# Four transformer-like layers on one core: loads, layer normalisation and some matmuls put in another order

## The chip, the cores and the metric

The kernel runs on one core of a Trainium2 chip. The metric is the time of one execution on the device, in microseconds (us), taken as the median of several executions. One execution of each kernel was also recorded by the hardware profiler; all readings of "the trace" and "the profile" below are from such single executions.

The engines are called as the profile calls them: PE is TensorE, DVE is VectorE, ACT is ScalarE, POOL is GpSimd, SP is the engine that issues the loads and stores (DMA). "L260" is a line of the kernel in question; the numbers differ from kernel to kernel.

## The reference

```python
S, D, F = 2048, 576, 4608            # bf16 inputs, 32 heads of 18

def A(x, wqkv, wo):                   # linear attention
    q, k, v = split(x @ wqkv)
    phi = lambda t: where(t > 0, t + 1, exp(t)) + 1e-6
    pq, pk = phi(q), phi(k)
    kv, z = einsum(pk, v), sum(pk)    # summed over all 2048 tokens
    return merge_heads(pq @ kv / (pq @ z + 1e-6)) @ wo

def B(x, w1, b1, w2, b2):             # MLP; it normalises its input once more
    return gelu(layernorm(x) @ w1 + b1) @ w2 + b2

x = x + A(layernorm(x), wqkv, wo)
x = x + B(layernorm(x), w1, b1, w2, b2)
x = x + A(layernorm(x), wqkv, wo)     # the same weights again
x = x + B(layernorm(x), w1, b1, w2, b2)
```

An attention layer has two passes, because `kv` needs all tokens before the first output can be made: a key/value pass (16 tiles of 128 tokens: normalise, transpose, project to k and v, accumulate), then a second pass (queries, output, projection with `wo`).

## The kernel before

All loads go through one queue, in the order of their issue by SP. Weights for later layers ("late pieces") are issued two per tile in the first key/value pass.

```python
load_x0(0); load_x0(1)
load_kd(wqkv_sb, A_wqkv, nc.sync)          # all three parts: q, k, v
load_x0(2); load_x0(3)
for i in range(NWARM):                     # 10 matmuls that only warm the clock
    nc.tensor.matmul(warm_ps[:], lhsT=ident[:], rhs=x0_tiles[0][:, 0:512], start=True, stop=True)
# ...
late_pieces = [piece_wo] + [w1 in 9 pieces] + [w2 in 6 pieces] + [piece_bias]   # abridged
#   piece_bias: load b1, cast it on DVE to b1T; load b2, cast it on DVE to b2_bc

def ln_part1(key, xt, kind, norm_eng):     # one tile's normalisation, all at once
    nc.vector.bn_stats(...); nc.vector.bn_stats(...); nc.vector.bn_aggr(...)    # ln_st, ln_mv
    nc.vector.tensor_scalar(...)                                                # ln_u = var + eps
    nc.gpsimd.tensor_tensor(out=rstd[:], in0=u[:], in1=neg_half[:], op=ALU.pow) # ln_rstd
    nc.vector.tensor_scalar(out=nmr[:], ...)                                    # ln_nmr = -mean * rstd
    # y_ring[...] = x * rstd + nmr on ACT (tiles 0 to 3) or POOL (the others)

def ln_part2(key, t, evac_eng):            # transpose, then copy out of PSUM
    # five PE transposes into tp (a single buffer), then
    # yT[..., t] = tp on DVE (first layer)

# key/value pass, first layer, before tile t:
#   load x of tile t+4, ln_part1 of tile t+4, ln_part2 of tile t+2, two late pieces
# kv_proj(t): PE k_ps -> ACT exp and identity -> DVE pk; PE v_ps -> ACT and DVE v_ring
# residual: two DVE additions of 288 columns each
```

v_ps is a single PSUM buffer. PE can write it for the next tile only after ACT and DVE have copied the last tile's value into v_ring.

## Time and profile before

| | before |
|---|---|
| median | 835.68 us (4 executions, 833.95 to 836.19) |
| profiled execution | 833.95 us, span 832.2 us, mean granted clock 0.995 |
| PE busy | 98% |

The first two parts of the page of the kernel before; the second line is the granted TensorE clock in tenths, in 40 slices of the span.

```profile
PE 813.1 (98%) x7154; PEld 672.7 (81%) x7154; DVE 297.1 (36%) x1034; ACT 410.1 (49%) x864; POOL 100.7 (12%) x148
...
PEclk8999999999999999999999999999999999999999
```

PE is the limit, and nearly all of its time is needed. So the question is where the other 2% lie, plus the time at a slow clock, which counts as busy. The view by windows of the kernel before, cut at the first key matmul (15.00 us), the start of the second pass (75.14), the first MLP's first output matmul (122.53) and the second attention layer's start (427.87):

```profile
core 0: us, PE busy (x) PEld busy (x) DVE busy (x) ACT busy (x) POOL busy (x), PEclk, DMA share, GB/s
0.00:15.00 15.00, 5.47 (x20) 2.55 (x21) 5.07 (x21) 3.23 (x4) 11.72 (x44) 0.90 0.90 280
15.00:75.14 60.14, 57.88 (x508) 45.21 (x506) 44.27 (x177) 37.90 (x94) 17.68 (x24) 0.97 0.74 204
75.14:122.53 47.39, 45.85 (x416) 34.36 (x416) 44.25 (x180) 31.79 (x56) 5.50 (x5) 1.00 0.43 139
122.53:427.87 305.34, 304.99 (x2716) 259.56 (x2714) 84.43 (x231) 134.83 (x283) 33.19 (x41) 1.00 0.14 45
```

Each row begins with its limits, then its length, then busy time by engine. The MLP row has 0.35 us to give; the first 75 us have the most.

The waits of PE in the first 128 us of the kernel before (who waited, for whom, sum, times, longest):

```profile
PE tp L186 <- DVE yT L190: 6.4, 1, 6.4
...
PE tp L186 <- POOL y_ring L178: 2.2, 3, 0.9
PE tp L186 <- ACT y_ring L174: 1.1, 2, 0.7
```

The large one is at the start. DVE's timeline of the kernel before shows why (start, length, what; the bracket is the idle time ahead of it and its end):

```profile
12.02 0.46 DVE L156 BATCH_NORM_STATS2 ln_st<-xbf 128x6 f32<-128x288 bf16 x1 [5.94 <-DMA xbf<-in_A_x_dram]
...
13.98 0.48 DVE L190 COPY yT<-tp 128x640 bf16<-128x640 bf16 x1
```

DVE stands 5.94 us in front of the third tile's statistics, because that tile's load is queued behind `wqkv`. The copy of the first transposed tile stands behind those statistics in DVE's order, and the second transpose, which needs the same PSUM buffer, waits for the copy. The Trainium skill says so in general ("TensorE: Matmul & The Clock Gate", Part 1, on engine queues): VectorE and ScalarE take their instructions strictly first in, first out. This trace agrees: the copy's input was ready at about 8 us (the first transposes start at 7.33) and it ran at 13.98 us.

### The profile page before, as it was taken

How to read it: one execution, taken by the hardware profiler on the slowest of the kernel's cores; microseconds unless marked ns; L12 is line 12 of the kernel's file. 1: busy time of each engine (PE TensorE's matmuls, PEld its weight loads, DVE VectorE, ACT ScalarE, POOL GpSimd, SP SyncE). 2: the span in 40 equal slices, each digit the busy share in tenths (PEclk: the TensorE clock that was granted, in tenths of full speed). 3: DMA queues.
4: the chain of work that ended last, by engine and by line, in shares of the span. 5: the costliest groups of instructions: out<-in, count | busy, mean ns of one | idle time of the engine just before them, and what ended most of it. 6: DMA issues, size and time to landing. Idle time of an engine off the chain costs nothing.

```text
span 832.2 us, 17608 instructions
## 1 busy us (share of the span) xinstructions
PE 813.1 (98%) x7154; PEld 672.7 (81%) x7154; DVE 297.1 (36%) x1034; ACT 410.1 (49%) x864; POOL 100.7 (12%) x148
## 2 busy tenths in 40 slices
PE   5989999999999999999999999999999999999998
PEld 3767688888888888888877867888888888888886
DVE  4777982324150505132134589551303010000000
ACT  3667653444444444444457776344444444444443
POOL 6330200112020202020000000211011010101000
PEclk8999999999999999999999999999999999999999
DMA  9970541202020202021010026721112010101010
GB/s 291 327 166 8 171 159 59 85 2 86 2 86 1 87 1 87 18 69 56 3 58 1 2 70 208 237 72 44 36 38 72 15 44 1 45 1 44 1 30 15
DMA packets 41009, 58.21 MB, mean 70 GB/s; under 512 B 7840, under 2 KB 24480, under 8 KB 40928
## 3 DMA queue, kind: packets, MB, share of 16 engines
q1 hardware_dynamic: 40928, 57.09, 22.2%
q8 instruction: 56, 0.92, 0.5%
q14 instruction: 25, 0.20, 0.1%
HBM read 40.56 MB, written 16.52 MB: 69 GB/s over the span
## 4 chain that ended last, share of the span: by engine, by line
PE 82%; issue 4%; DVE 4%; DMA 1%; POOL 1%; POOLq 0%; ACT 0%; DVEq 0%; SPq 0%
PE h_ps L421 34%; PE m_ps L406 30%; PE wo_ps L374 4%; PE q_ps L278 4%; PE k_ps L246 3%; PE tp L186 2%; PE v_ps L257 2%; PE v_ps L254 1%; PE to_ps L364 1%; PE nd_ps L329 1%; POOL ln_rstd L167 1%; PE kvacc L270 1%; DMA xo<-x_d 1%; DVE xn L227 1%; DVE y_ring L178 1%
## 5 line engine op out<-in xcount | busy, mean ns | idle before, releaser
L424 ACT ACTIVATE hT<-h_ps,b1T 128x256 bf16<-128x256 f32 x576 | 273.2, 474 | 340.2 <-PE h_ps L421 333.2
L421 PE MATMUL h_ps<-yT,w_sb 128*128 128x256 bf16 x2880 | 407.5, 273 | 0.0
L406 PE MATMUL m_ps<-w_sb,hT 128*128 128x288 bf16 x2304 | 370.4, 286 | 0.0
L421 PEld LDWEIGHTS <-w_sb 128*128 128x128 bf16 x2880 | 279.5, 98 | 44.6
L406 PEld LDWEIGHTS <-hT 128*128 128x128 bf16 x2304 | 225.4, 98 | 42.6
L190 DVE COPY yT<-tp 128x640 bf16<-128x640 bf16 x60 | 29.1, 486 | 273.5 <-PE tp L186 273.4
L167 POOL TENSOR_TENSOR ln_rstd<-ln_u,neg_half 128x1 f32<-128x1 f32 x64 | 36.2, 566 | 504.0 <-DVE ln_u L162 273.7
L216 POOL TENSOR_TENSOR xo<-xo,b_bc 128x576 f32<-128x576 f32 x32 | 44.7, 1403 | 185.4 <-DMA xo<-x_d 185.4
L278 PE MATMUL q_ps<-yT,wqkv_sb 128*126 128x512 bf16 (+1 forms) x200 | 53.8, 381 | 0.0
L374 PE MATMUL wo_ps<-wo_sb,oT 128*128 128x288 bf16 x320 | 46.4, 286 | 0.1
L246 PE MATMUL k_ps<-wqkv_sb,yT 128*128 128x288 bf16 x320 | 46.3, 291 | 0.0
L227 DVE TENSOR_TENSOR xn<-m_ps,xo 128x288 f32<-128x288 f32 x32 | 13.3, 437 | 76.5 <-PE m_ps L406 76.5
L186 PE MATMUL tp<-ident,y_ring 128*128 128x128 bf16 x320 | 29.3, 224 | 11.4 <-DVE yT L190 6.7
L374 PEld LDWEIGHTS <-oT 128*128 128x128 bf16 x320 | 30.8, 98 | 9.9 <-ACT oT L366 1.0
L186 PEld LDWEIGHTS <-y_ring 128*128 128x128 bf16 x320 | 22.9, 100 | 19.4 <-issue 7.9
L227 DVE TENSOR_TENSOR xbf<-m_ps,xo 128x288 bf16<-128x288 f32 x32 | 12.4, 450 | 68.9 <-issue 35.7
L246 PEld LDWEIGHTS <-yT 128*128 128x128 bf16 x320 | 30.3, 99 | 7.7
L178 DVE TENSOR_SCALAR y_ring<-xn,ln_rstd,ln_nmr 128x576 bf16<-128x576 f32 x44 | 35.1, 798 | 0.6
L199 ACT ACTIVATE phi_e<-q_ps 126x512 bf16<-126x512 f32 (+1 forms) x40 | 23.9, 596 | 22.3 <-PE q_ps L278 19.8
L199 ACT ACTIVATE phi_e<-k_ps 128x288 bf16<-128x288 f32 x64 | 26.6, 416 | 11.2 <-PE k_ps L246 7.4
L202 DVE TENSOR_SCALAR phi_e<-phi_e 128x288 bf16<-128x288 bf16 (+2 forms) x104 | 27.7, 268 | 11.3 <-ACT phi_e L199 11.3
L278 PEld LDWEIGHTS <-wqkv_sb 128*126 128x126 bf16 (+1 forms) x200 | 23.8, 131 | 8.2
(70 smaller groups left out, 530.9 us busy)
## 6 DMA issues: line engine op xcount, KB each, us to landing
x_d<-xn SPq DMA_DIRECT2D x48, 288.0 KB, 2.2
xo<-x_d SPq DMA_DIRECT2D x48, 288.0 KB, 3.0
xn<-x_d SPq DMA_DIRECT2D x28, 288.0 KB, 3.3
w_sb<-in_B_w_dram SPq DMA_DIRECT2D x6, 864.0 KB, 9.3
xbf<-in_A_x_dram SPq DMA_DIRECT2D x32, 144.0 KB, 2.8
w_sb<-in_B_w_dram SPq DMA_DIRECT2D x9, 512.0 KB, 6.8
out_dram<-xbf SPq DMA_DIRECT2D x16, 144.0 KB, 1.8
wqkv_sb<-in_A_wqkv_dram SPq DMA_DIRECT2D x1, 1728.0 KB, 9.0
```

The source lines that it names most:

```text
L167: nc.gpsimd.tensor_tensor(out=rstd[:], in0=u[:], in1=neg_half[:], op=ALU.pow)
L178: eng.tensor_scalar(out=y[:, 0:D], in0=xt[:, 0:D], scalar1=rstd[:, 0:1], scalar2=nmr[:, 0:1], op0=ALU.mult, op1=ALU.add)
L186: nc.tensor.transpose(out=tp[:, k, :], in_=y[:, k * P:(k + 1) * P], identity=ident[:])
L199: nc.scalar.activation(out=e[0:rows, 0:n], in_=ps_ap, func=ACT.Exp)
L216: nc.gpsimd.tensor_tensor(out=xo[:], in0=xo[:], in1=b2_bc[:], op=ALU.add)
L227: nc.vector.tensor_tensor(out=xn[:, half * HALF:(half + 1) * HALF], in0=halves[half], in1=xo[:, half * HALF:(half + 1) * HALF], op=ALU.add)
L246: nc.tensor.matmul(kp[:, 0:HALF], lhsT=yT[:, k, tok], rhs=wqkv_sb[:, k, D + half * HALF: D + (half + 1) * HALF], start=(k == 0), stop=(k = ...
L278: nc.tensor.matmul(qp[0:GR[g], :], lhsT=wqkv_sb[:, k, GO[g]:GO[g] + GR[g]], rhs=yT[:, k, c * CA:(c + 1) * CA], start=(k == 0), stop=(k == ...
L374: nc.tensor.matmul(wp[:, half, 0:HALF], lhsT=oT[:, k, :], rhs=wo_sb[:, k, half * HALF:(half + 1) * HALF], start=(k == 0), stop=(k == KD - 1))
L406: nc.tensor.matmul(accs[j][:, half, 0:HALF], lhsT=hT[:, j * P:(j + 1) * P], rhs=w2_sb[:, f, half * HALF:(half + 1) * HALF], start=(f == 0) ...
L421: nc.tensor.matmul(hp[:, 0:CB], lhsT=w1_sb[:, k, f * P:(f + 1) * P], rhs=yT[:, k, ctok], start=(k == 0), stop=(k == KD - 1))
L424: nc.scalar.activation(out=hT[:], in_=hp[:, 0:CB], func=ACT.Gelu_apprx_tanh, bias=b1T[:, f:f + 1], scale=1.0)
```

## The change

The change intends to let matmuls start earlier and to keep DVE and POOL from making PE wait in the first attention layer. Its core, with cuts:

```diff
-NWARM = 10
+NWARM = 14
+# every start-up load is chained to the one before it, so that the scheduler keeps the order
-        load_x0(0)
-        load_x0(1)
-        load_kd(wqkv_sb, A_wqkv, nc.sync)
-        load_x0(2)
-        load_x0(3)
+        for t in range(6):
+            load_x0(t)                                  # six x buffers instead of four
+        chained(nc.sync.dma_start(out=wqkv_sb[:, 0:4, D:3 * D], ...))   # k and v columns only
+        chained(nc.sync.dma_start(out=wqkv_sb[0:64, 4, D:3 * D], ...))
-            nc.tensor.matmul(warm_ps[:], lhsT=ident[:], rhs=x0_tiles[0][:, 0:512], ...)
+            nc.tensor.matmul(warm_ps[:], lhsT=ident[:], rhs=y_ring[NY - 1][:, 0:512], ...)
-        late_pieces = [piece_wo] + [w1 ...] + [w2 ...] + [piece_bias]          # two per tile
+        late_pieces = [piece_q, piece_wo] + [w1 ...] + [w2 ...] + [piece_b1_dma]  # one per tile
+        # b2 is loaded four tiles before the end of the pass; both casts at the last tile:
+        def bias_casts():
+            nc.vector.tensor_copy(out=b1T[:], in_=bias_stage.pop("b1")[:])
+            nc.vector.tensor_copy(out=b2_bc[:], in_=bias_stage.pop("b2")[:])
-        def ln_part1(...) / def ln_part2(...)
+        class LNPipe:          # one stage of each tile per tick:
+            # 0 statistics, 1 ln_rstd, 2 ln_nmr, 3 y_ring, 4 transpose and copy
+            # stage 0 of later tiles: bn_stats ordered after the last value copy (state['vcopy'])
-            ln_part2 of the first layer: copy on DVE, two tiles ahead
+            feed(x0_tiles.pop(k), k, "A", l0_norm_eng(k), "act")   # copy on ACT, fed five tiles ahead
-            for half in range(2): nc.vector.tensor_tensor(... 288 columns ...)
+            nc.vector.tensor_tensor(... 576 columns in one ...)
             while q0:
                 q_proj(*q0.pop(0))
+            q_proj(0, 1)       # two query projections moved ahead of the second pass
+            q_proj(1, 1)
+        # up to eight of the MLP's first products (h_ps) are issued in the attention's last four tiles
```

The diff shows the order of the program. When the kernel is built, a scheduler orders each engine's instructions once more, and the traces show where it differs.

## The prediction

> **What bounds the kernel now.** TensorE. The page shows PE busy 813.1 of 832.2 us (98%). In the timeline, matmuls follow each other at 109 ns (256 columns) and 122 ns (288 columns) through both MLP layers. Summing that steady spacing over all matmuls after the warm-up gives about 801 us (estimate from the trace). So only some 30 us of the span can move at all:
> - Start-up: the first key projection (k_ps) starts at 15.00 us, and the window view grants only half the clock from about 13 to 19.8 us (k_ps spaced 240 ns). About 2 us of the work after 15 us is lost to that.
> - First attention layer, key/value pass: 2.9 us of PE gaps, 2.6 of them before transposes (tp) at 49, 55 and 58 us, waiting for POOL's y_ring.
> - Its second pass: about 2.8 us. Second attention layer: about 2.1 + 1.6 us. MLP layers: about 1 us.
> - Tail: 4.3 us after the last matmul starts.
>
> **What the change does.** It reorders. Matmul work is the same but for 4 more warm-up matmuls. It
> 1. loads six x tiles and only the K and V columns of wqkv first,
> 2. moves layer 0's yT evacuations from VectorE (486 ns) to ScalarE (693 ns),
> 3. cuts LayerNorm into stages spread over ticks,
> 4. emits two q projections early and up to 8 MLP products ahead,
> 5. merges the two residual adds (437 ns each) into one (estimate 0.75 us).
>
> **Start-up, costed.** Before, VectorE sits 5.94 us in front of tile 2's statistics, because that tile's load queued behind wqkv (landed after 9.0 us); the evacuation of tile 0 stands behind them, so tp waits 6.4 us for it. That wait goes. But the instruction order of the new kernel puts all six tiles' statistics ahead of the first ln_nmr. At about 0.91 us a tile from 3.02 us, ln_nmr of tile 0 comes near 8.6 us (5.35 before). ScalarE then does four normalisations (0.81 us apart) before the first evacuation, near 12.1 us; the second transpose waits for it, and k_ps starts near 13.2 us. So the start gains about 1.8 us, not the 5 us that the DMA order (K,V landed near 9.3 us, estimate) would allow. PE is idle from about 9 to 12.8 us except for one transpose group, so the clock may drop again. The Trainium skill ("TensorE: Matmul & The Clock Gate", Part 1) says that the clock is halved until a busy window of about 3.4 us; the trace agrees (warm-up matmuls 427 ns apart[...]). I count 1.2 us of the 2.
>
> **The sum.** Start -1.8, clock -1.2, y_ring gaps -2.2 (x tiles come six ahead, VectorE loses an evacuation per tile), second pass -1.4, MLP -0.5, second attention layer -1.3, tail -0.1: about -8.5 us. ScalarE gains 16 x 0.69 us off the critical path (66% busy at 20 to 40 us).
>
> **Predicted: 827 us, 80% range 821 to 832.** Faster by over 2%: 0.03; within 2%: 0.955; slower by over 2%: 0.015.
>
> **What would show it.** Timeline: first k_ps at 12.5 to 14 us; first ln_nmr near 8.6 us; the four normalisations ahead of the first yT copy. Waits: no tp waiting over 0.5 us for y_ring at 49 to 60 us. MLP stages within 0.5 us of before. PE busy again at 98% or more.
>
> **What would make it wrong.** If k_ps starts near 10 us with a full clock, the time falls to about 822 us. If ScalarE, now holding the evacuations behind its exponentials, makes PE wait for the single tp buffer, the key/value pass loses what it gained. If the x loads, now chained behind weight pieces, hold VectorE at statistics, the first attention layer gets longer.

## The result

| | before | after |
|---|---|---|
| median | 835.57 us (16 executions, 833.24 to 839.05) | 830.82 us (11 executions, 829.78 to 832.51) |
| profiled execution | 833.95 us, span 832.2 | 829.44 us, span 827.7 |

The ratio of after to before is 0.994, with a 95% interval of 0.9927 to 0.9953. A ratio here is the mean time of one kernel's runs over that of the other's of the same rounds, so it is not quite the ratio of the medians quoted. The chip was not the same in all batches (the kernel before had medians of 834.9, 836.64 and 835.98 us in the three batches of experiments), so experiments are best compared by their ratios to before.

The view by windows of the changed kernel, cut at the same events:

```profile
0.00:12.67 12.67, 6.18 (x25) 2.66 (x25) 6.82 (x32) 5.00 (x6) 10.10 (x37) 0.92 0.72 220
12.67:72.62 59.95, 58.60 (x508) 45.79 (x507) 39.38 (x152) 45.28 (x108) 20.23 (x25) 0.96 0.85 233
72.62:122.10 49.48, 48.91 (x440) 36.73 (x440) 44.08 (x166) 33.91 (x59) 5.62 (x5) 1.00 0.40 133
122.10:423.68 301.58, 301.58 (x2690) 257.02 (x2688) 79.08 (x213) 133.00 (x280) 35.76 (x41) 1.00 0.14 44
```

The start is 2.33 us shorter, the key/value pass only 0.19 us. The other rows can't be compared by length, as the change moved matmuls from the MLP (2716 to 2690) to the second pass (416 to 440). For that I sum, over the matmuls of a stage, the distance to the next matmul less N/2.4 + 2.5 ns for N columns. That is the full-rate spacing which the Trainium skill gives ("TensorE: Matmul & The Clock Gate", Part 1); the traces agree (109 ns at 256 columns, 122 ns at 288). What is left is pauses and slow clock. It goes from 5.40 to 5.00 us in the first key/value pass, from 2.68 to 2.01 in its second pass, from 1.02 to 0.22 in the first MLP, from 2.17 to 1.93 and from 1.41 to 1.30 in the second attention layer, and from 0.06 to 0.22 in the last MLP.

The waits of PE in the first 128 us of the changed kernel:

```profile
PE tp L240 <- ACT yT L242: 2.4, 1, 2.4
PE v_ps L311 <- DVE v_ring L318: 1.3, 2, 1.0
PE tp L240 <- ACT y_ring L228: 1.0, 1, 1.0
PE to_ps L425 <- DVE o_ring L404: 0.5, 1, 0.5
```

The waits for POOL's y_ring are gone. The start went as the prediction had it: ACT's timeline of the changed kernel has four normalisations ahead of the first copy,

```profile
8.42 3.14 ACT L228 ACTIVATE y_ring<-xbf,ln_nmr,ln_rstd 128x576 bf16<-128x576 bf16 x4 [4.04 <-DVE ln_nmr L220]
11.46 0.67 ACT L242 COPY yT<-tp 128x640 bf16<-128x640 bf16 x1
```

and PE's timeline of the changed kernel has the second group of transposes, released by that copy, and the first key matmul:

```profile
12.18 0.69 PE L240 MATMUL tp<-ident,y_ring 128*128 128x128 bf16 x5 [2.39 <-ACT yT L242]
12.67 1.65 PE L303 MATMUL k_ps<-wqkv_sb,yT 128*128 128x288 bf16 x6
```

But there is a new wait of v_ps for v_ring, and DVE's timeline of the changed kernel shows a stop that the kernel before does not have:

```profile
56.54 0.31 DVE L262 TENSOR_TENSOR pk<-phi_a,phi_e 128x288 bf16<-128x288 bf16 x1
58.51 0.18 DVE L171 CAST b1T<-b_raw 128x36 f32<-128x36 bf16 x1 [1.66 <-DMA b_raw<-in_B_b_dram]
58.61 0.23 DVE L260 TENSOR_SCALAR phi_e<-phi_e 128x288 bf16<-128x288 bf16 x1
```

The same place in DVE's timeline of the kernel before, where the cast follows without a stop:

```profile
53.50 0.44 DVE L157 BATCH_NORM_STATS2 ln_st<-xbf 128x6 f32<-128x288 bf16 x1
53.98 0.18 DVE L143 CAST b1T<-b_raw 128x36 f32<-128x36 bf16 x1
```

The load of b1 is 9 KB, but it is the last in a queue of weights, and it goes as 4608 packets of 2 bytes. It landed at 53.96 us before and at 58.49 us after: 4.5 us later, while the computation runs 2.3 us earlier. By the packets' times, the changed kernel's load was issued at 45.46 us, its first packet started at 52.49 us, its last ended at 56.04 us, and 2.4 us later it had landed. The view by windows of the changed kernel shows the queue ahead of these packets and while they run (the last number is GB/s):

```profile
44.40:52.40 8.00, 7.50 (x68) 5.72 (x67) 5.97 (x22) 7.17 (x18) 3.43 (x4) 1.00 1.09 356
52.40:56.10 3.70, 3.15 (x30) 2.53 (x30) 2.75 (x11) 2.33 (x6) 1.50 (x2) 1.00 1.17 69
```

Before, it was issued 2.0 us earlier and waited 4.0 us for its first packet, not 7.0. The traces show one reason for the delay: in the changed kernel the load of the seventh x tile is not issued before 9.31 us, since its buffer is free only when tile 0 is normalised, and all later loads are chained behind it. From 8 to 12 us the queue moved 197 GB/s, before the change 319. No run isolates this, and none loads b1 earlier or in larger packets.

In this execution the stop at 58.5 us itself costs PE little: the pauses of v_ps are at 51.6 us (1.17 us) and 55.8 us (0.45 us), ahead of it. They stand with the other thing that makes DVE stop, ln_nmr waiting up to 0.67 us a tile for POOL's ln_rstd. This stop is not new. DVE's waits from 15 to 72 us, in the kernel before and then in the changed kernel:

```profile
DVE ln_nmr L169 <- POOL ln_rstd L167: 5.8, 12, 0.7
DVE ln_nmr L220 <- POOL ln_rstd L216: 6.0, 10, 0.7
```

What is new is that PE waits for v_ps behind it. But this profiled execution is the fastest of the twelve of the changed kernel, and it ran 4.83 us after its first key matmul at half clock, so it came late to the b1 load. Would an execution that comes earlier wait longer? The times fit that: the three executions at the lowest mean clock (0.995) took 829.44, 829.78 and 830.13 us, the four at the highest (0.998) 829.96 to 831.76 us, so a fuller clock brought no time.

### The profile page after: what moved, and what is told of

It is laid out like the page before. It is cut to its first block, busy times and chain, and to the rows that moved or that the text cites. A ratio compares the mean times of both kernels' runs of the same rounds, so it can differ in the third digit from the quotient of the medians.

```text
span 827.7 us, 17553 instructions
## 1 busy us (share of the span) xinstructions
PE 814.5 (98%) x7158; PEld 673.4 (81%) x7158; DVE 286.4 (35%) x955; ACT 420.1 (51%) x880; POOL 104.5 (13%) x141
## 4 chain that ended last, share of the span: by engine, by line
PE 87%; issue 4%; DVE 1%; DMA 0%; ACT 0%; POOLq 0%; DVEq 0%; POOL 0%; SPq 0%
PE h_ps L469 36%; PE m_ps L486 32%; PE wo_ps L435 5%; PE q_ps L335 4%; PE k_ps L303 3%; PE tp L240 2%; PE v_ps L314 2%; PE v_ps L311 1%; PE to_ps L425 1%; PE nd_ps L390 1%; PE kvacc L327 1%; DMA xo<-x_d 0%; POOLq L626 0%; DVE xn L284 0%; DVE xbf L284 0%
## 5 line engine op out<-in xcount | busy, mean ns | idle before, releaser
L469 PE MATMUL h_ps<-yT,w_sb 128*128 128x256 bf16 x2880 | 403.0, 273 | 0.0
L244 DVE COPY yT<-tp 128x640 bf16<-128x640 bf16 x44 | 21.6, 490 | 241.5 <-PE tp L240 241.5
L435 PE MATMUL wo_ps<-wo_sb,oT 128*128 128x288 bf16 x320 | 52.3, 286 | 0.0
L335 PE MATMUL q_ps<-yT,wqkv_sb 128*126 128x512 bf16 (+1 forms) x200 | 51.5, 381 | 0.0
L284 DVE TENSOR_TENSOR xn<-m_ps,xo 128x576 f32<-128x576 f32 x16 | 11.4, 753 | 92.9 <-PE m_ps L486 92.9
L284 DVE TENSOR_TENSOR xbf<-m_ps,xo 128x576 bf16<-128x576 f32 x16 | 11.4, 752 | 87.8 <-PE m_ps L486 51.9
L427 ACT COPY oT<-to_ps 128x640 bf16<-128x640 bf16 x32 | 22.1, 691 | 19.3 <-PE to_ps L425 19.0
L232 DVE TENSOR_SCALAR y_ring<-xn,ln_rstd,ln_nmr 128x576 bf16<-128x576 f32 x44 | 31.2, 709 | 0.6
```

The costliest lines, as they stand in the source:

```text
L232: eng.tensor_scalar(out=y[:, 0:D], in0=xt[:, 0:D], scalar1=it["rstd"][:, 0:1], scalar2=it["nmr"][:, 0:1], op0=ALU.mult, op1=ALU.add)
L335: nc.tensor.matmul(qp[0:GR[g], :], lhsT=wqkv_sb[:, k, GO[g]:GO[g] + GR[g]], rhs=yT[:, k, c * CA:(c + 1) * CA], start=(k == 0), stop=(k == ...
L435: nc.tensor.matmul(wp[:, half, 0:HALF], lhsT=oT[:, k, :], rhs=wo_sb[:, k, half * HALF:(half + 1) * HALF], start=(k == 0), stop=(k == KD - 1))
L469: nc.tensor.matmul(hp[:, 0:CB], lhsT=w1_sb[:, k, f * P:(f + 1) * P], rhs=yT[:, k, ctok], start=(k == 0), stop=(k == KD - 1))
```

## The experiments

The theories were these. (1) What the change gains at the start it partly gives back, since DVE, which works in order, stops in the key/value pass for the bias load and for POOL. (2) Rivals: the start is limited by ACT's new copies or by the clock, and removing those limits gives the whole gain; or the moves in the second pass don't give what I had counted.

Twelve kernels ran, in three batches; all gave correct results. Each is an edit of the changed kernel. In the first batch (3 rounds) the kernel before had a median of 834.9 us.

### evac_dve: the first layer's copies back on DVE

```diff
-            lnp.feed(x0_tiles.pop(t), t, "A", l0_norm_eng(t), "act")
+            lnp.feed(x0_tiles.pop(t), t, "A", l0_norm_eng(t), "dve")
```
(the same for the tiles fed in the pass)

> The changed kernel, with layer 0's yT evacuations back on VectorE. Theory (the order of VectorE's queue decides the start): the first evacuation now stands behind the statistics of tile 6, whose load lands at about 12.4 us, so the first k_ps moves from 12.67 to about 13.9 us, and the key/value pass of layer 0 gets no shorter: about 1 to 3 us slower than the changed kernel (831.8 to 834), ratio to the kernel before 0.996 to 0.998. Rival (ScalarE's four normalisations alone hold the start): k_ps at about 11.5 us and 1 us or more faster than the changed kernel.

Measured: 831.93 us (830.1 to 832.45, 4 executions), ratio 0.9955 (0.9928 to 0.9982). The first key matmul starts at 13.87 us, 1.2 us later than in the changed kernel: the second transposes wait 3.6 us for DVE's copy. The v_ps matmuls then pause 2.65 us at 57.4 us, where DVE stands 4.2 us for b1, which lands at 59.53 us. So ACT's copies are worth about a microsecond at the start. The two pauses of v_ps at 51.6 and 55.8 us, which the changed kernel has, are absent here. The time itself differs from the changed kernel's by less than the intervals allow to tell.

### warm26: 26 warm-up matmuls instead of 14, from a buffer of their own

```diff
-NWARM = 14
+NWARM = 26
-        nc.vector.memset(y_ring[NY - 1][:], 0.0)
+        warm_src = const.tile([P, 512], BF16, name="warm_src")
+        nc.vector.memset(warm_src[:], 0.0)
+        nc.vector.memset(y_ring[NY - 1][:, D:DPAD], 0.0)
-            ... rhs=y_ring[NY - 1][:, 0:512] ...
+            ... rhs=warm_src[:] ...
```

> The changed kernel with 26 warm-up matmuls on a tile of their own instead of 14 on y_ring 3. They fill TensorE to about 10.8 us and need nothing that the start-up chain needs. Theory (the dip of the clock is a cost of its own): k_ps still starts at 12.5 to 12.9 us, no half clock after about 7.3 us, k_ps spaced 122 ns from the first one; 1.9 to 2.6 us faster than the changed kernel, ratio to before 0.991. Rival (with a full clock PE only waits for VectorE and ScalarE in those first tiles): clock full but under 1 us gained.

Measured: 836.73 us (834.71 to 837.5, 4 executions), ratio 1.0013 (0.9985 to 1.0041): as slow as the kernel before, though it did what it was to do. Its first key matmul starts at 12.68 us, as in the changed kernel, and at the full clock. The key/value pass then took 66.6 us instead of 59.95. DVE's timeline of warm26:

```profile
55.80 0.31 DVE L264 TENSOR_TENSOR pk<-phi_a,phi_e 128x288 bf16<-128x288 bf16 x1
59.92 0.18 DVE L173 CAST b1T<-b_raw 128x36 f32<-128x36 bf16 x1 [3.81 <-DMA b_raw<-in_B_b_dram]
60.01 0.23 DVE L320 CAST v_ring<-v_ps 128x72 bf16<-128x72 f32 x1
```

PE's timeline of warm26, at the same place:

```profile
60.29 1.21 PE L313 MATMUL v_ps<-wqkv_sb,yT 128*128 128x252 bf16 x5 [4.27 <-DVE v_ring L320]
```

Here the copy that frees v_ps stands behind the cast. And the stop is paid twice: the view by windows of warm26 grants half the clock in the two stretches after it (the column after POOL).

```profile
55.91:59.32 3.41, 0.11 (x1) 0.00 (x0) 0.20 (x1) 0.86 (x3) 0.00 (x0) 1.00 0.60 121
59.32:62.73 3.41, 2.44 (x11) 1.63 (x11) 1.22 (x6) 0.00 (x0) 0.00 (x0) 0.50 0.46 139
62.73:66.14 3.41, 3.41 (x22) 2.48 (x21) 0.72 (x3) 1.98 (x4) 0.00 (x0) 0.50 0.00 0
```

There was another stop of v_ps, 2.08 us at 46.5 us, where DVE waited 2.5 us for the b2 load. An earlier, faster computation meets loads that are no earlier.

### front2: the first two tiles served first

The first two tiles go through all stages before the statistics of tiles 2 to 5 (both halves) and before their normalisations; POOL's clearing of padding comes after its first ln_rstd.

```diff
-        for t in range(LEAD):
-            ...
+        for t in range(2):
+            lnp.feed(x0_tiles.pop(t), t, "A", l0_norm_eng(t), "act")
+        lnp.drain()
+        for t in range(2, LEAD):
             lnp.feed(x0_tiles.pop(t), t, "A", l0_norm_eng(t), "act")
+            lnp.items[-1]['after'] = state['nmr1']        # statistics after tile 1's ln_nmr
+            lnp.items[-1]['norm_after'] = state['evac1']  # normalisation after tile 1's copy
             lnp.tick()
+        ...                                           # two more ticks
```

> The changed kernel with tiles 0 and 1 put first on VectorE and ScalarE: their ln_nmr before the statistics of tiles 2 to 5, their evacuations before normalisations 2 and 3. Loads as in the changed kernel. Theory (queue order first, then the landing of the K and V columns): ln_nmr of tile 0 near 5.4 us, both evacuations done by about 10.2 us, k_ps then waits for the weights that landed at 11.5 and 12.2 us in the changed kernel: k_ps at 11.5 to 12.2 us, 0.5 to 1.2 us gained, clock as before or better. Rival (queue order is all): k_ps near 10 us, 2.5 us or more gained.

Measured: 829.6 us (828.95 to 831.92, 4 executions), ratio 0.9936 (0.9908 to 0.9965), the same as the changed kernel. The first key matmul came at 11.88 us, now held by the k and v weights (landed at 11.84 us), and the clock stayed full to the end of the work. Yet the pass ended at 72.72 us, in the changed kernel at 72.62. PE's waits from 10 to 75 us in front2:

```profile
PE v_ps L317 <- DVE v_ring L324: 3.9, 2, 3.0
PE k_ps L309 <- DMA wqkv_sb<-in_A_wqkv_dram: 2.4, 1, 2.4
```

All that was saved at the start was lost at 56 us, where DVE stood 4.7 us for b1.

### front2_x4: front2 with the k and v weights ahead of x tiles 4 and 5

```diff
-        for t in range(6):
+        for t in range(4):
             load_x0(t)
         ... k and v columns of wqkv ...
+        for t in range(4, 6):
+            load_x0(t)
```
(and the statistics of tiles 4 and 5 come after tile 3's ln_nmr)

> As front2, and the loads of tiles 4 and 5 behind the K and V columns. Theory (both limits lifted): weights land about 1 us sooner than in front2 (10.3 to 11.2 us), k_ps follows at 10.3 to 11.3 us, TensorE's gap before it is under 1.5 us, so the clock stays full in most runs: 3 to 5 us faster than the changed kernel, ratio to before 0.988 to 0.991. Rival (the weights' last packets land near 11.5 us whatever stands before them): k_ps at 11.5 us and over, clock dips, 1 us or less.

Measured: 831.6 us (831.27 to 834.88, 4 executions), ratio 0.9968 (0.9932 to 1.0004). The first key matmul starts at 10.30 us, the earliest of all runs, and the pass ends at 74.68 us, 2 us later than in the changed kernel. v_ps pauses 1.25, 1.07 and 2.82 us at 45.6, 49.9 and 56.9 us, and half clock follows from 60.9 to 64.3 us. Over these four kernels the first key matmul ranges from 10.3 to 13.9 us, and the end of the pass does not follow it.

### bias_late: both casts after the key/value pass

In the second batch (5 rounds) the kernel before had a median of 836.64 us.

```diff
             kv_acc(NT - 1)
+            bias_casts()          # and made to depend on state['vcopy']
             while q0:
...
-                bias_casts()      # taken out of the last tile
```

> The changed kernel with one alteration: the two bias casts on VectorE (b1T, b_bc) are issued after the first layer's key/value pass instead of inside it. Theory: in the changed kernel VectorE, which works in order, stands 1.66 us at 58.5 us until the small b1 load has landed, and spends 0.93 us on the b_bc cast at 46.5 us; both delay the v_ring casts and so the v_ps matmuls (pauses of 1.17 us at 51.6 us and 0.45 us at 55.8 us). Taking them out should end the key/value pass 0.5 to 1.4 us earlier (72.6 to about 71.6 us), time about 829.8 us (829.4 to 830.4). Rival: those pauses come from VectorE waiting for GpSimd's ln_rstd alone, then the two pauses stay as they are and the time stays within 0.4 us of 830.8 us.

Measured: 831.04 us (829.89 to 833.87, 6 executions), ratio 0.9938 (0.9922 to 0.9954): no gain. The pauses of v_ps were 0.89 and 0.44 us, so the rival was right about them: they stay without the casts. The pass took 59.59 us, 0.36 less than in the changed kernel, but the second pass and the MLP behind it together took 1.06 us more (352.11 against 351.05). The built kernel explains that this is not a clean experiment: the edit had also moved matmuls (268 lines of difference in PE's list). Its trace also has one reload of x that took 4.10 us where about 2.7 is usual there, and 2.2 us of pause in the last MLP behind it.

### front2_bias: front2 with the same edit

> The kernel front2 (first two tiles' normalisation served first, full clock, first key matmul at 11.9 us, yet no faster than the changed kernel) with the bias casts after the key/value pass. Theory: whatever is saved at the start is given back at 54 to 59 us, where VectorE stands 4.65 us for the b1 load, which lands at a time set by the load queue (58.4 to 60 us in all runs) and not by the computation; then the 3.1 us pause of v_ps at 56.3 us goes, and the time falls to about 826.3 us (825.5 to 827.2), 3 to 4 us below front2. Rival: the key/value pass is held by the arrival of the x tiles and weights in general; then the pause moves to the transposes or key matmuls and the time stays at 829 to 830 us.

Measured: 829.08 us (828.6 to 830.19, 5 executions), ratio 0.9912 (0.99 to 0.9925). The pause of 3.1 us went, as the theory said; the pass ended at 70.75 us instead of 72.72, though 3.41 us of half clock followed the first key matmul here and none in front2. Of that, 1.4 us came back in the second pass and the MLP (352.22 us together, 350.84 in front2), as in bias_late. The expected time was not reached.

### front2_best: front2_bias, with POOL's tiles having ln_nmr on POOL

```diff
-                        nc.vector.tensor_scalar(out=nmr[:], ...)
+                        nmr_eng = nc.gpsimd if it["norm"] == "pool" else nc.vector
+                        nmr_eng.tensor_scalar(out=nmr[:], ...)
```

> front2_bias, and the shift ln_nmr of the tiles that GpSimd normalises is computed on GpSimd, so VectorE no longer waits 0.4 to 0.7 us for ln_rstd in each of 10 tiles. Theory: the remaining v_ps pause of about 1.1 us at 49 us comes from these waits ahead of the pk and v_ring work, so another 0.5 to 1.2 us goes: 825.4 us (824.6 to 826.4). Rival: GpSimd becomes the later one (rstd about 0.55 us, shift about as much, normalisation about 1 us a tile every 3.4 us), its y_ring tiles arrive later and the transposes wait: same as front2_bias or up to 1 us slower.

Measured: 829.45 us (826.12 to 830.12, 6 executions), ratio 0.9909 (0.9892 to 0.9927). The last pause of v_ps, 0.49 us in front2_bias, is gone; the time can't be told from front2_bias's.

### no_ahead: without the two moves that fill the second pass

```diff
-            q_proj(0, 1)
-            q_proj(1, 1)
...
-                    if c == 1 and g < 2:
-                        continue
...
-                if 12 <= s <= 15:
+                if False and 12 <= s <= 15:
```
(and 8 instead of 12 buffers for the MLP's products)

> The changed kernel without the two moves that fill the second half of attention: the two query projections before the bridge, and the eight MLP groups issued in its last four tiles. My prediction had put 1.4 us on the first layer's second pass, 0.5 us on the MLPs and part of 1.3 us on the second attention layer. Accounted from the traces of before and after, the two moves brought 0.67 (second pass, first layer) + 0.11 (second layer) + 0.8 (first MLP) - 0.16 us. If that accounting holds, this run is 1.0 to 1.8 us slower than the changed kernel: 832.3 us (831.6 to 832.9). If the moves only shift pauses from one stage to another, it is within 0.5 us of 830.8 us; if my prediction's terms were right and something else took them back, it is 2.5 us slower or more, about 833.5 us.

Measured: 830.64 us (829.9 to 834.14, 6 executions), ratio 0.9935 (0.9919 to 0.9952), against 0.994 (0.9927 to 0.9953) with the moves. So the two moves did not pay 2.5 us; the 1.4 us that the traces of before and after put on them (0.67 + 0.11 + 0.80 - 0.16) was not confirmed either. The difference of the ratios is worth 0.4 us in favour of leaving the moves out, and the intervals leave nearly 2 us of room either way. Below that this experiment is inconclusive in time. Its trace says more about single terms. The first MLP has 0.08 us of pauses and slow clock without the moves (1.02 before, 0.22 with them), so the 0.80 us is not theirs. The second pass has 2.86 us (2.68 before, 2.01 with them), but the kernels that share the changed kernel's order of matmuls there range from 1.47 to 2.55. As 35 query matmuls precede the second pass here too, the first of the two moves was hardly tested.

### bias_pin: the casts held back in DVE's order, nothing else moved

In the third batch (5 rounds) the kernel before had a median of 835.98 us. The built list of bias_pin differs from that of the changed kernel in the places of the two casts on DVE and in nothing else on PE, ACT, DVE and POOL. The order in the two traces agrees.

```diff
         def bias_casts():
-            nc.vector.tensor_copy(out=b1T[:], in_=bias_stage.pop("b1")[:])
-            nc.vector.tensor_copy(out=b2_bc[:], in_=bias_stage.pop("b2")[:])
+            for dst, key in ((b1T, "b1"), (b2_bc, "b2")):
+                cast = nc.vector.tensor_copy(out=dst[:], in_=bias_stage.pop(key)[:])
+                tc.add_manual_dep(cast.ins, state['vcopy'].ins.name, NOSYNC, reason='casts late in the key/value pass')
```

> The changed kernel; the two bias casts are held in VectorE's order until after the value copy of the last tile but one. By the built order, nothing else moves on TensorE, ScalarE or GpSimd (the earlier bias_late also reordered 268 rows of TensorE's list, in the second pass, which I take for the reason why it won 0.5 us in the key/value pass and lost 1.1 us after it). Theory: the b1 load lands at about 58.5 us whatever the computation does, and the cast that waits for it in the middle of the pass holds v_ps; then the 0.45 us pause goes, the 1.17 us pause ahead of it shrinks to 0.3 to 0.8, the pass ends 0.6 to 1.4 us earlier, time about 829.9 us if the chip is as for the changed kernel, ratio to before 0.9928. Rival: these pauses belong to VectorE's waits for ln_rstd; pass and time unchanged, ratio 0.994.

Measured: 828.39 us (827.53 to 829.59, 5 executions), ratio 0.9912 (0.99 to 0.9924), clear of the changed kernel's 0.9927 to 0.9953: 0.0028 of 835 us, or 2.3 us, for moving two small casts (the ends of the intervals leave 0.3 to 4.4 us; the changed kernel itself was not run again in this batch). DVE's timeline of bias_pin has the casts without a stop:

```profile
66.25 0.17 DVE L172 CAST b1T<-b_raw 128x36 f32<-128x36 bf16 x1
66.33 0.45 DVE L172 CAST b_bc<-xbf 128x576 f32<-128x576 bf16 x1
```

b1, landed at 60.02 us, has no one waiting for it. The expectation had the size too small and one detail wrong: the pauses of v_ps stayed at 0.92 and 0.45 us, so the casts don't make these two. ln_rstd is the likely cause, as DVE stops 0.67 us for it ahead of each; that is argued, and evac_dve, which has neither pause, says that the order of the copies plays a part. In the two profiled executions the difference of the spans is 1.9 us, of which about 1.1 us is luck with the clock (2.68 instead of 4.83 us at half clock behind the first key matmul, and half of that difference is lost), 0.25 us is v_ps and 0.5 us lies in the second pass. That the gain of the medians is larger than what this pair of traces shows fits with executions that come earlier and wait longer; but there is no trace of a slower execution of the changed kernel, so this part is argued from the times above and from warm26, front2, front2_x4 and evac_dve.

### warm26_pin: warm26 with the same edit

> The kernel warm26 (26 warm-up matmuls, first key matmul at 12.68 us at the full clock, yet 835.3 us span) with the bias casts held back in the same way. Theory: warm26 lost 2.1 us at 46.5 us to the b2 load, 4.4 us at 55.7 us to the b1 load, and then 3.4 us of 6.8 us at half clock from 59.3 us, which followed that stop; all of it goes, the key/value pass takes 57 to 58 us instead of 66.6, and the time falls by 8 to 9.5 us to about 827.5 us (826.3 to 828.7), ratio about 0.9905. Rival: the additional warm-ups themselves cost later clock; then a half-clock stretch stays, without a stop ahead of it, and the time stays above 830 us.

Measured: 829.07 us (828.37 to 830.56, 6 executions), ratio 0.9926 (0.9914 to 0.9937). The same edit brought 0.0087, or 7.3 us. PE's timeline of warm26_pin, where warm26 had stopped:

```profile
56.80 0.70 PE L314 MATMUL v_ps<-wqkv_sb,yT 128*128 128x252 bf16 x5
```

The pass took 57.45 us instead of 66.6, at the full clock. So the casts in the pass, not the warm-ups, were what made warm26 slow. The full clock made it no faster than bias_pin, though: in its trace 1.1 us came back in the second pass, where a residual addition waits 0.92 us for the store that frees its buffer, and 0.8 us in the last MLP.

### front2_pin and best_pin

front2_pin is front2 with the edit of bias_pin; best_pin has ln_nmr on POOL as well, as in front2_best. PE's and ACT's lists are those of front2 in both.

> The kernel front2 with the bias casts held back in the same way (TensorE's order identical to front2's). Theory: of front2's pauses of 1.07 us at 49.2 us and 3.13 us at 56.3 us, the second goes, the first stays or halves; the second pass stays as in front2, since the order is the same; time 829.6 less 3.1 to 3.6, about 826.2 us (825.2 to 827.2), ratio about 0.9895, if the clock stays full as it did in front2's profiled run; if 3.4 us at half clock fall behind the first key matmul, 1.7 us more. Rival: the pass is held by the loads of x as well, then transposes wait and the time is 828 us or more.

Measured for front2_pin: 827.8 us (827.09 to 829.46, 5 executions), ratio 0.9905 (0.9893 to 0.9917). That is 2.6 us better than front2 by the ratios. The expected size was reached only in part; the first key matmul came at 12.54 us here, 0.66 us later than in front2's trace, and 3.41 us of half clock followed.

> front2_pin with the shift ln_nmr of GpSimd's tiles computed on GpSimd, so that VectorE no longer waits 0.4 to 0.7 us a tile for ln_rstd. Theory: the remaining v_ps pause of about 1 us at 49 us goes: 0.5 to 1 us under front2_pin, about 825.5 us (824.4 to 826.8), ratio about 0.9885. Rival: it is hidden by the six tiles' lead, no difference to front2_pin within 0.5 us.

Measured for best_pin: 825.98 us (825.51 to 827.56, 4 executions), ratio 0.9886 (0.9873 to 0.9898). PE's waits from 10 to 75 us in best_pin, to be set against those of front2:

```profile
PE k_ps L311 <- DMA wqkv_sb<-in_A_wqkv_dram: 1.1, 1, 1.1
PE tp L248 <- ACT yT L250: 0.8, 1, 0.8
```

No wait for v_ring is left, and the pass took 57.72 us with 3.41 us of half clock in it. The step from front2_pin is 0.0019 or 1.6 us; the two intervals overlap by a hair (0.9893 to 0.9898). In the two traces the spans differ by 2.2 us, of which only 0.5 us lies in the pass, where the v_ps pause was; 0.7 us is an earlier first key matmul and 1.0 us lies behind the pass. The same edit made no difference between front2_bias and front2_best. So moving ln_nmr takes the pause away, but its worth in time is not shown. best_pin is the fastest kernel, about 9.5 us (1.14%) faster than before, and its interval is clear of the changed kernel's.

| kernel | first k_ps | end of pass | v_ps pauses, 45 to 61 us | median | ratio to before |
|---|---|---|---|---|---|
| after | 12.67 | 72.62 | 1.6 | 830.82 | 0.9940 |
| evac_dve | 13.87 | 74.97 | 2.7 | 831.93 | 0.9955 |
| warm26 | 12.68 | 79.29 | 7.7 | 836.73 | 1.0013 |
| front2 | 11.88 | 72.72 | 4.5 | 829.60 | 0.9936 |
| front2_x4 | 10.30 | 74.68 | 5.1 | 831.60 | 0.9968 |
| bias_pin | 12.78 | 71.26 | 1.4 | 828.39 | 0.9912 |
| warm26_pin | 12.53 | 69.98 | 1.3 | 829.07 | 0.9926 |
| front2_pin | 12.54 | 70.79 | 0.5 | 827.80 | 0.9905 |
| best_pin | 11.87 | 69.59 | 0 | 825.98 | 0.9886 |

## Why the prediction was right or wrong

The predicted time, 827 us with a range of 821 to 832, holds the measured 830.82 us, and the class (within 2%) was right. But the range was 11 us wide, more than the whole gain that was forecast; its middle was missed by 3.8 us. The mechanism at the start was right too: the order of the statistics, the four normalisations ahead of the first copy, the second transposes waiting for it. But the sum was -8.5 us and the result -4.75 us. By terms, measured as stage excess in the two traces:

| term of the prediction | predicted | traces |
|---|---|---|
| start | -1.8 | -2.33 |
| clock | -1.2 | +0.5 |
| y_ring gaps (rest of the key/value pass) | -2.2 | -0.9 |
| second pass | -1.4 | -0.67 |
| MLP | -0.5 | -0.64 |
| second attention layer | -1.3 | -0.35 |
| tail | -0.1 | -0.06 |
| sum | -8.5 | -4.45 |

- **Start.** First k_ps at 12.67 us (said: 12.5 to 14, estimate 13.2); first ln_nmr at 8.22 us (said: near 8.6). The DMA limit beneath it was misjudged: I took k and v to land near 9.3 us, and they landed at 11.49 and 12.17 us. So with this order of loads there were not 5 us to be had but hardly more than 1, as front2 showed (11.88 us, held by these weights); with two x tiles behind the weights, front2_x4 came to 10.30 us.
- **Clock.** In this pair of traces the term had the wrong sign, and it is the largest miss of the table. 3.85 us of half clock followed the first key matmul before (to 18.85 us; the prediction had read 19.8), 4.83 us after (half of that is lost). That is partly luck: the mean granted clock is 0.9966 over the changed kernel's twelve executions and 0.9945 over the 29 of the kernel before in the three batches, so over all executions it did rise. How much time that was worth can't be read from a mean, which also counts half clock without work. The prediction itself had said that PE, idle from 9 to 12.8 us, might lose the clock again, and still counted a gain. The Trainium skill warns in the same section that the window is free-running and the number of cold matmuls varies from run to run; these runs agree: the mean granted clock of the changed kernel's twelve executions ranged from 0.995 to 0.998, and over all traces 0 to 4.83 us of half clock followed the first key matmul at the start. A term like this should be an expected value over the phases with a range, not a gain.
- **y_ring gaps.** They went as predicted, but I had counted only the wait that goes and no wait that comes: in the traces 2.65 us of pauses before tp went and 1.62 us before v_ps came. DVE took over the role of POOL: it stops for ln_rstd, no longer than before, and for the bias loads, and v_ps now waits behind it. bias_pin shows 2.3 us for the bias casts by the ratios, the greater part of the 3.75 us that were missing in the medians. The rest is not shown by an experiment; the step from front2_pin to best_pin tests ln_rstd on another start and within the noise. The prediction's last sentence had named the right kind of risk (loads chained behind weights holding DVE), for the x loads instead of b1.
- **Second pass, MLP.** Half of the first and all of the second are in the traces, but the second is not due to the MLP products issued ahead: no_ahead's first MLP gains as much without them. What else in the change brings it is open. no_ahead rules out that the two moves are worth 2.5 us in the time itself; what they bring in the second pass stays open. In bias_pin's trace the excess of the second pass is 1.47 us, 1.2 us under before, near the predicted 1.4.
- **Second attention layer.** The waits of tp for y_ring fell from 1.3 us (0.9 for DVE's, 0.4 for ACT's) to 0.8 us, not to nothing. I had taken the normalisation's new stages to hide all of it. No experiment was spent on it, so why 0.8 us stays is open.
- **What would show it.** "No tp waiting over 0.5 us for y_ring at 49 to 60 us" held, and was not enough: the sign had to be that PE waits for nothing there. PE busy stayed at 98%. "MLP stages within 0.5 us of before" did not hold: the first MLP lost 0.80 us of pauses.

## What to carry to other kernels

When work is moved earlier, ask of every load that an in-order engine consumes in the middle of the hot loop when it lands: loads at the end of a full queue do not come earlier, and a 0.18 us cast of 9 KB can hold the copy that frees a single PSUM buffer. The load of b1 was slow to move as well: its packets of 2 bytes took 3.6 us. Keep such casts out of the loop, or order them behind the last thing that others wait for, and compare the built instruction order to be sure that nothing else moved. In a prediction, list the waits that the new order creates beside those that it removes.

## What the Trainium skill lacked or had wrong

- "TensorE: Matmul & The Clock Gate", Part 1, says that the clock falls after at least one idle window of about 3.4 us. Here a window need not be idle throughout. In evac_dve the window before the fall had 0.92 us of PE busy, in warm26 0.11 us. Over all fourteen traces, cut along these windows, the busiest window with a fall behind it had 1.52 us (changed kernel, 7.26 to 10.68 us), and the least busy one after which the clock stayed full had 1.50 us (warm26, 45.66 to 49.08 us). So the limit lay near 1.5 us of PE busy in these runs, transposes counted. Windows of evac_dve, then of front2, where a longer stop (3.13 us) was split over two windows with 2.16 and 1.71 us busy and the clock stayed full:

```profile
57.42:60.83 3.41, 0.92 (x9) 0.64 (x8) 1.17 (x6) 0.98 (x4) 0.00 (x0) 1.00 0.92 250
60.83:64.24 3.41, 3.41 (x22) 2.56 (x20) 1.39 (x5) 0.58 (x1) 0.00 (x0) 0.50 0.02 6
```

```profile
54.42:57.84 3.42, 2.16 (x23) 1.71 (x22) 0.00 (x0) 2.48 (x6) 0.00 (x0) 1.00 0.58 74
57.84:61.25 3.41, 1.71 (x19) 1.49 (x19) 1.44 (x7) 0.28 (x1) 0.00 (x0) 1.00 0.68 187
```

- The same page gives one busy window, sustained for about 3.4 us, as enough to free the clock, and not how busy it has to be. In warm26 the window from 59.32 to 62.73 us had 2.44 us of PE busy and the next one still ran at 0.50. In no_ahead the window from 12.09 to 15.50 us had 2.65 us and the next one ran at 1.00. So between 2.44 and 2.65 us busy is where one such window began to count in these runs.
- No page that I read has how long a small load waits at the end of a busy queue: here the 9 KB of b1 took 10.5 us from issue to landing before the change, and 13.0 us after, of which 7.0 us passed before its first packet started and 3.6 us while its 2-byte packets ran.
